# Decode attention with a gated MLP on one core: sums over d moved from VectorE to TensorE, K and V on one queue, MLP weights last

## The chip, the cores and the metric

The kernel runs on one core of a Trainium2 chip. The metric is the device time of one execution in microseconds (us). Each kernel is run several times beside the kernel before on the same chip; all runs quoted here are of the fast state (none lies over 1.5% above the fastest of its kernel), except two single looks whose state is unknown (they are marked). A profile is one more execution, recorded by the hardware profiler; its "span" is about 2 us shorter than the measured time.

Names: PE is TensorE, PEld its weight loads, DVE is VectorE, ACT is ScalarE, POOL is GpSimd, SP is the sync engine that issues DMA transfers. L327 is line 327 of the kernel.

## The reference, cut to what matters

```python
# B=2 sequences, one new token each; D=512, 32 heads, Sk=8192 cached positions, Dh=128, F=1376, bf16
h  = x + attention(layernorm(x), k_cache, v_cache, wq, wo)   # softmax(q k^T / sqrt(Dh)) v, per head
h2 = h + (relu(g) * u) @ W_down       # g, u = layernorm(h) @ W_gate, layernorm(h) @ W_up
```

There are 64 (sequence, head) pairs, called heads below. Each reads a K tile and a V tile of 2.1 MB and uses every element once. Together with wq, wo (4.2 MB each) and the MLP weights (4.2 MB), the core reads 281 MB.

## The kernel before

Position s = p*64 + j lies in partition p. For each head VectorE multiplies the K tile by q (copied to all partitions), then sums over d by halving: four tree adds down to 8 values per position and one reduce. ScalarE takes exp, and TensorE forms the weighted sum of V with 64 one-column matmuls.

```python
NB = 3                                    # three buffers for K (SP queue), three for V (ACT queue)
for i in range(NH):                       # 64 heads
    nc.vector.tensor_tensor(out=prod[:], in0=kt[buf][:], in1=qb, op=ALU.mult)        # L327
    # ... SP reloads kt[buf] for head i+3; wo is loaded at head 5
    while cur_w > 8:                      # 128 -> 64 -> 32 -> 16 -> 8
        half = cur_w // 2
        nc.vector.tensor_tensor(out=out_ap, in0=cur_in[:, :, 0:half],
                                in1=cur_in[:, :, half:cur_w], op=ALU.add)            # L349
        # ...
    nc.vector.tensor_reduce(out=scores[par][:], in_=cur_in, axis=AX.X, op=ALU.add)   # L358
    nc.scalar.activation(out=e_t[par][:], in_=scores[par][:], func=ACT.Exp, ...)
    for j in range(64):
        nc.tensor.matmul(O_ps[:, col:col + 1], lhsT=vt[buf][:, j, :], rhs=e_t[par][:, j:j + 1], ...)  # L377
# MLP weights go into K and V buffers freed near the end; then softmax sums, output projection of
# all 32 heads, layernorm, gate, up, down, a transpose to rows, store.
```

The softmax here doesn't subtract the row's maximum and nothing guards it: scores larger than these inputs give would overflow.

Of the kernel before, what the change touches and what calls it, by code (L numbers as in the profile page):

```python
# [13 lines left out]
class EngChain:  # L14

    def __init__(self, eng, sem):
        self.eng = eng
        self.sem = sem
        self.count = 0
        self.pending = False  # L20

    def wait(self):
        if self.pending:
            self.eng.wait_ge(self.sem, self.count)
            self.pending = False

    def run(self, inst):
        inst.then_inc(self.sem, 1)
        self.count += 1
        self.pending = True  # L30
        return inst


def bass_sequential_preLN__gqa_block_cached__glu_gated_reglu__decode_kernel(
# [11 lines left out]
):  # L46
    B, _, D = A_x.shape
    _, Hkv, Sk, Dh = A_k_cache.shape
    Hq = A_wq.shape[1] // Dh
    assert Hq == Hkv  # L50
    assert Dh == 128
    assert D % 128 == 0
    DC = D // 128
    J = Sk // 128
    assert Sk % 128 == 0 and J >= 2 and (J & (J - 1)) == 0
    F = B_W_gate.shape[1]
    FC = (F + 127) // 128
    NH = B * Hq
    inv_sqrt_dh = 1.0 / math.sqrt(Dh)
    eps = 1e-5  # L60
    qdim = Hq * Dh
    GH = 4 if Hq % 4 == 0 else Hq
    NGB = Hq // GH
    NG = B * NGB
    GW = GH * Dh
    assert GW <= 512
    NB = 3

    with ExitStack() as es:
# [3 lines left out]
        sem_x = S("x")  # L73
        sem_wo = S("wo")
        sem_wgu = S("wgu")
        sem_wd = S("wd")
        sem_prep = S("prep")
        sem_stats = S("stats")
        sem_lnx = S("lnx")
        sem_qps = S("qps")  # L80
        sem_qcopied = S("qcopied")
        kdone = [S(f"kdone{k}") for k in range(NB)]
        vdone = [S(f"vdone{k}") for k in range(NB)]
        multdone = S("multdone")
        sready = S("sready")
        expdone = S("expdone")
        pvdone = S("pvdone")
        sem_ident0 = S("ident0")
        sem_ident = S("ident")
        sem_z = S("ztok")  # L90
        sem_zinv = S("zinv")
        sem_zb = S("zb")
        sem_osb = S("osb")
        sem_attn = S("attn")
        sem_hprep = S("hprep")
        sem_hstats = S("hstats")
        sem_hn = S("hn")
        sem_gu = S("gu")
        sem_hd = S("hd")
        sem_y = S("ysem")  # L100
        sem_h2 = S("h2sem")
        sem_rows = S("rowsem")
        sem_rowsb = S("rowsbsem")
        osem = S("osem")
        dvesem = S("dvechain")
        sem_sq1a = S("sq1a")
        sem_sq1b = S("sq1b")
        sem_sq2a = S("sq2a")
        sem_sq2b = S("sq2b")

        dve = EngChain(nc.vector, dvesem)
        actsem = S("actchain")
        actc = EngChain(nc.scalar, actsem)

        kt = [es.enter_context(nc.sbuf_tensor(f"kt{i}", [128, J, Dh], BF16)) for i in range(NB)]
        vt = [es.enter_context(nc.sbuf_tensor(f"vt{i}", [128, J, Dh], BF16)) for i in range(NB)]
        wq_sb = es.enter_context(nc.sbuf_tensor("wq_sb", [128, DC, qdim], BF16))
        xrep = es.enter_context(nc.sbuf_tensor("xrep", [128, B * DC, 128], BF16))
        q_grp = [es.enter_context(nc.sbuf_tensor(f"qgrp{i}", [128, GW], BF16)) for i in range(2)]
        wo_sb = es.enter_context(nc.sbuf_tensor("wo_sb", [128, Hq, D], BF16))  # L120
        ones_f32 = es.enter_context(nc.sbuf_tensor("ones_f32", [128, 128], F32))
        ident_f32 = es.enter_context(nc.sbuf_tensor("ident_f32", [128, 128], F32))
        xT = es.enter_context(nc.sbuf_tensor("xT", [128, DC, B], BF16))
        xT_f = es.enter_context(nc.sbuf_tensor("xT_f", [128, DC * B], F32))
        xsq = es.enter_context(nc.sbuf_tensor("xsq", [128, DC * B], F32))
        sumb = es.enter_context(nc.sbuf_tensor("sumb", [128, B], F32))
        sumq = es.enter_context(nc.sbuf_tensor("sumq", [128, B], F32))
        mean = es.enter_context(nc.sbuf_tensor("mean", [128, B], F32))
        msq = es.enter_context(nc.sbuf_tensor("msq", [128, B], F32))
        var = es.enter_context(nc.sbuf_tensor("var", [128, B], F32))  # L130
        rstd = es.enter_context(nc.sbuf_tensor("rstd", [128, B], F32))
        vareps = es.enter_context(nc.sbuf_tensor("vareps", [128, B], F32))
        sqv = es.enter_context(nc.sbuf_tensor("sqv", [128, B], F32))
        lnxT = es.enter_context(nc.sbuf_tensor("lnxT", [128, DC, B], BF16))
        hT_f = es.enter_context(nc.sbuf_tensor("hT_f", [128, DC * B], F32))
        hsq = es.enter_context(nc.sbuf_tensor("hsq", [128, DC * B], F32))
        hnT = es.enter_context(nc.sbuf_tensor("hnT", [128, DC, B], BF16))
        hd = es.enter_context(nc.sbuf_tensor("hd", [128, FC * B], BF16))
        h2T_f = es.enter_context(nc.sbuf_tensor("h2T_f", [128, DC * B], F32))
        rows_sb = es.enter_context(nc.sbuf_tensor("rows_sb", [DC * B, 128], BF16))  # L140
        zinv = es.enter_context(nc.sbuf_tensor("zinv", [1, NH], F32))
        ZP = es.enter_context(nc.sbuf_tensor("ZP", [128, NH], F32))
        zb_sb = es.enter_context(nc.sbuf_tensor("zb_sb", [128, NH], F32))
        u_sb = es.enter_context(nc.sbuf_tensor("u_sb", [128, FC * B], F32))
        O_sb = es.enter_context(nc.sbuf_tensor("O_sb", [128, Hq, B], BF16))
        prod = es.enter_context(nc.sbuf_tensor("prod", [128, J, Dh], BF16))
        tb1 = es.enter_context(nc.sbuf_tensor("tb1", [128, J * 64], BF16))
        scores = [es.enter_context(nc.sbuf_tensor(f"scores{i}", [128, J], F32)) for i in range(2)]
        e_t = [es.enter_context(nc.sbuf_tensor(f"e{i}", [128, J], BF16)) for i in range(2)]

        if DC * F <= J * Dh and FC * D <= J * Dh and NH >= 3:
            alias_w = True
            pstride = kt[0][:].ap[0]
            wg_view = bass.AP(kt[(NH - 3) % NB], 0, [[pstride[0], 128], [F, DC], [1, F]])
            wu_view = bass.AP(kt[(NH - 2) % NB], 0, [[pstride[0], 128], [F, DC], [1, F]])
            wd_view = bass.AP(vt[(NH - 3) % NB], 0, [[pstride[0], 128], [D, FC], [1, D]])
        else:
            alias_w = False
            wg_t = es.enter_context(nc.sbuf_tensor("wg_sb", [128, DC, F], BF16))
            wu_t = es.enter_context(nc.sbuf_tensor("wu_sb", [128, DC, F], BF16))  # L160
            wd_t = es.enter_context(nc.sbuf_tensor("wd_sb", [128, FC, D], BF16))
            wg_view = wg_t[:]
            wu_view = wu_t[:]
            wd_view = wd_t[:]

        qps = es.enter_context(nc.psum_tensor("qps", [128, 2 * 512], F32))
        work = es.enter_context(nc.psum_tensor("work", [128, 512], F32))
        O_ps = work[:, 0:NH]
        zrow_ps = work[0:1, 64:64 + NH]
        zb_ps = work[:, 128:128 + NH]  # L170
        msum_ps = work[:, 192:192 + DC * B]
        e2_ps = work[:, 200:200 + DC * B]
        attnT_ps = work[:, 208:208 + DC * B]
        hsum_ps = work[:, 216:216 + DC * B]
        hsq_ps = work[:, 224:224 + DC * B]
        g_ps = work[:, 232:232 + FC * B]
        u_ps = work[:, 254:254 + FC * B]
        yT_ps = work[:, 276:276 + DC * B]
        rows_ps = work[0:DC * B, 288:288 + 128]

        NWQ = NGB
        sem_wq = [S(f"wq{k}") for k in range(NWQ)]
        nfull = F // 128
        frem = F - nfull * 128

        def dma_wq_chunk(k):
            return nc.sync.dma_start(  # L187
                wq_sb[:, :, k * GW:(k + 1) * GW],
                A_wq[:, k * GW:(k + 1) * GW].rearrange("(c p) n -> p c n", p=128),
            ).then_inc(sem_wq[k], 16)  # L190

        def dma_k(i):
            b, h = divmod(i, Hq)
            return nc.sync.dma_start(  # L194
                kt[i % NB][:], A_k_cache[b, h].rearrange("(p j) d -> p j d", p=128)
            ).then_inc(kdone[i % NB], 16)
# [7 lines left out]
        def emit_q_group_pe(g):  # L204
# [4 lines left out]
            if g >= 2:  # L209
                nc.tensor.wait_ge(sem_qcopied, g - 1)  # L210
# [9 lines left out]
        def emit_q_group_copy(g):  # L220
            slot = g % 2
            nc.scalar.wait_ge(sem_qps, g + 1)
            if g >= 2:
                nc.scalar.wait_ge(multdone, (g - 1) * GH)
# [321 lines left out]
```

## Time and profile before

| | before |
|---|---|
| time | 710.18 us (median of 4) |
| K multiply starts: head 0, 1, 61, 63 | 27.4, 41.6, 658.8, 678.8 us |
| end of the span | 708.4 us |

From the page of the kernel before: busy time of each engine; then, in 40 slices of 17.7 us, the busy share in tenths of VectorE and of the DMA engines, and the rate; then the line of instruction fetches (packets, MB, share).

```profile
span 708.4 us, 9878 instructions
PE 158.7 (22%) x4433; PEld 130.2 (18%) x4433; DVE 630.6 (89%) x424; ACT 34.4 (5%) x149; POOL 0.7 (0%) x6
DVE  0679998299999999999999999999999999999982
DMA  9999999999999999999999999999999999999940
GB/s 345 367 426 427 425 417 392 423 396 384 426 424 421 421 418 427 409 409 424 420 425 422 422 413 424 422 412 423 428 427 409 420 424 417 420 417 416 401 162 3
q8 instruction: 35, 0.57, 0.3%
```

VectorE and DMA are both busy nearly all the time. The rate is low in the first two slices, and in the slice that begins 35 us before the end loading is nearly over while VectorE still works. The chain of work that ended last, by engine, says which of the two rules:

```profile
DVE 84%; DMA 8%; SPq 4%; PE 2%; issue 2%; DVEq 0%; ACT 0%
```

One head in the middle of the run (timeline: start, duration, engine, line, operation):

```profile
338.57 4.43 DVE L327 TENSOR_TENSOR prod<-kt,qgrp 128x8192 bf16<-128x8192 bf16 x1
343.04 2.29 DVE L349 TENSOR_TENSOR tb<-prod 128x4096 bf16<-128x4096 bf16 x1
345.36 1.22 DVE L349 TENSOR_TENSOR prod<-tb 128x2048 bf16<-128x2048 bf16 x1
346.62 0.69 DVE L349 TENSOR_TENSOR tb<-prod 128x1024 bf16<-128x1024 bf16 x1
347.34 0.42 DVE L349 TENSOR_TENSOR prod<-tb 128x512 bf16<-128x512 bf16 x1
347.80 0.69 DVE L358 TENSOR_REDUCE scores<-prod 128x64 f32<-128x512 bf16 x1
348.58 4.43 DVE L327 TENSOR_TENSOR prod<-kt,qgrp 128x8192 bf16<-128x8192 bf16 x1
```

VectorE works without a gap: 10.0 us from one K multiply to the next. A head moves 4.19 MB, so this alone allows 419 GB/s. The 16 KB packets of the trace mostly take 611 ns on each of 16 DMA engines, or 429 GB/s. The two limits are 2 to 3% apart.

### The profile page before, as it was taken

The page shows a single profiled execution, that of the slowest core. Times are in us where ns is not written, and L with a number is a line of the kernel's source. Part 1 is how long each engine was busy: PE and PEld are TensorE (multiplying, and loading weights), DVE is VectorE, ACT ScalarE, POOL GpSimd, SP SyncE. Part 2 cuts the span into 40 slices and gives each one's busy share as a digit, 9 for nine tenths or more (in the row PEclk, how much of TensorE's full clock was granted, in tenths as well). Part 3 has the DMA queues.
Part 4 walks back from the last instruction along what each step waited for, and adds up shares of the span by engine and source line. Part 5 has one row for each costly group of instructions (what it writes and reads, how often), then busy time and mean ns, then how long its engine had stood idle before and what let it go on. Part 6 is the DMA issues. An engine that isn't in the chain of part 4 may idle for free.

```text
span 708.4 us, 9878 instructions
## 1 busy us (share of the span) xinstructions
PE 158.7 (22%) x4433; PEld 130.2 (18%) x4433; DVE 630.6 (89%) x424; ACT 34.4 (5%) x149; POOL 0.7 (0%) x6
## 2 busy tenths in 40 slices
PE   0221322011323132212322132122322232112215
PEld 0111222011222122212221122112221222112215
DVE  0679998299999999999999999999999999999982
ACT  0100000000000000000000000000000000000010
POOL 0000000000000000000000000000000000000000
DMA  9999999999999999999999999999999999999940
GB/s 345 367 426 427 425 417 392 423 396 384 426 424 421 421 418 427 409 409 424 420 425 422 422 413 424 422 412 423 428 427 409 420 424 417 420 417 416 401 162 3
DMA packets 30346, 281.70 MB, mean 398 GB/s; under 512 B 3328, under 2 KB 12896, under 8 KB 13920
## 3 DMA queue, kind: packets, MB, share of 16 engines
q1 hardware_dynamic: 21088, 146.84, 49.9%
q10 hardware_dynamic: 9216, 134.22, 46.1%
q8 instruction: 35, 0.57, 0.3%
q14 instruction: 7, 0.06, 0.0%
HBM read 281.05 MB, written 0.00 MB: 397 GB/s over the span
## 4 chain that ended last, share of the span: by engine, by line
DVE 84%; DMA 8%; SPq 4%; PE 2%; issue 2%; DVEq 0%; ACT 0%
DVE prod L327 38%; DVE tb L349 25%; DVE prod L349 14%; DMA kt<-in_A_k_cache_dram 8%; DVE scores L358 6%; SPq L194 2%; SPq L187 2%; PE work L422 1%; PE work L377 0%; PE work L464 0%; DVEq L323 0%; PE work L470 0%; PE work L494 0%; SPq L247 0%; ACT e L363 0%
## 5 line engine op out<-in xcount | busy, mean ns | idle before, releaser
L327 DVE TENSOR_TENSOR prod<-kt,qgrp 128x8192 bf16<-128x8192 bf16 x64 | 283.3, 4426 | 29.5 <-DMA kt<-in_A_k_cache_dram 20.8
L377 PE MATMUL work<-e,vt 128*128 128x1 bf16 x4096 | 119.5, 165 | 517.7 <-ACT e L363 517.7
L377 PEld LDWEIGHTS work<-e,vt 128*128 128x128 bf16 x4096 | 114.3, 104 | 535.2 <-ACT e L363 535.2
L349 DVE TENSOR_TENSOR tb<-prod 128x4096 bf16<-128x4096 bf16 (+1 forms) x128 | 190.9, 1491 | 4.4
L349 DVE TENSOR_TENSOR prod<-tb 128x2048 bf16<-128x2048 bf16 (+1 forms) x128 | 105.6, 825 | 4.4
L363 ACT ACTIVATE e<-scores 128x64 bf16<-128x64 f32 x64 | 16.4, 256 | 630.8 <-DVE scores L358 630.8
L358 DVE TENSOR_REDUCE scores<-prod 128x64 f32<-128x512 bf16 x64 | 43.9, 686 | 2.2
L213 PE MATMUL qps<-wq_sb,xrep 128*128 128x512 bf16 x64 | 29.9, 623 | 4.4 <-DVEq L303 3.3
L262 DVE CAST xT_f<-xT 128x8 f32<-128x8 bf16 x1 | 0.2, 172 | 19.0 <-DMA xT<-in_A_x_dram 19.0
L363 ACT ACTIVATION_READ_ACCUMULATOR e<-scores 128x1 f32 x64 | 11.9, 186 | 0.0
L213 PEld LDWEIGHTS qps<-wq_sb,xrep 128*128 128x128 bf16 x64 | 6.9, 128 | 14.2 <-issue 8.8
L226 ACT ACTIVATE qgrp<-qps 128x512 bf16<-128x512 f32 x16 | 9.3, 579 | 4.0 <-PE qps L213 4.0
L268 PE MATMUL work<-xT_f,ones_f 128*128 128x8 f32 x2 | 0.6, 372 | 20.4 <-DVE xsq L264 20.4
L268 PEld LDWEIGHTS work<-xT_f,ones_f 128*128 128x128 f32 x2 | 0.5, 310 | 20.4 <-DVE xsq L264 20.4
L422 PE MATMUL work<-O_sb,wo_sb 128*128 128x2 bf16 x128 | 3.6, 165 | 0.6 <-DVEq L416 0.6
L422 PEld LDWEIGHTS work<-O_sb,wo_sb 128*128 128x128 bf16 x128 | 3.5, 104 | 0.8 <-DVEq L416 0.8
L427 DVE TENSOR_TENSOR hT_f<-work,xT_f 128x8 f32<-128x8 f32 x1 | 0.2, 167 | 3.7 <-PE work L422 3.7
L475 DVE COPY u_sb<-work 128x20 f32<-128x20 f32 x1 | 0.2, 178 | 3.1 <-PE work L470 3.1
L403 DVE RECIPROCAL zinv<-work 1x64 f32<-1x64 f32 x1 | 0.5, 547 | 2.6 <-PE work L399 2.6
L464 PE MATMUL work<-hnT,kt 128*128 128x2 bf16 (+1 forms) x44 | 1.5, 170 | 2.1 <-DVEq L457 2.1
L464 PEld LDWEIGHTS work<-hnT,kt 128*128 128x128 bf16 (+1 forms) x44 | 1.5, 112 | 2.2 <-DVEq L457 2.2
L470 PE MATMUL work<-hnT,kt 128*128 128x2 bf16 (+1 forms) x44 | 1.5, 170 | 0.0
(53 smaller groups left out, 21.0 us busy)
## 6 DMA issues: line engine op xcount, KB each, us to landing
vt<-in_A_v_cache_dram ACTq DMA_DIRECT2D x64, 2048.0 KB, 13.0
kt<-in_A_k_cache_dram SPq DMA_DIRECT2D x64, 2048.0 KB, 13.6
wq_sb<-in_A_wq_dram SPq DMA_DIRECT2D x8, 512.0 KB, 11.4
wo_sb<-in_A_wo_dram SPq DMA_DIRECT2D x1, 4096.0 KB, 41.8
kt<-in_B_W_gate_dram SPq DMA_DIRECT2D x1, 1376.0 KB, 10.9
kt<-in_B_W_up_dram SPq DMA_DIRECT2D x1, 1376.0 KB, 6.5
vt<-in_B_W_down_dram SPq DMA_DIRECT2D x1, 1280.0 KB, 9.0
vt<-in_B_W_down_dram SPq DMA_DIRECT2D x1, 96.0 KB, 9.2
```

The lines of the kernel that those rows point to most:

```text
L187: return nc.sync.dma_start(wq_sb[:, :, k * GW:(k + 1) * GW], A_wq[:, k * GW:(k + 1) * GW].rearrange("(c p) n -> p c n", p=128),).then_inc( ...
L194: return nc.sync.dma_start(kt[i % NB][:], A_k_cache[b, h].rearrange("(p j) d -> p j d", p=128)).then_inc(kdone[i % NB], 16)
L213: last = nc.tensor.matmul(qps[:, slot * 512:slot * 512 + GW], lhsT=xrep[:, b_g * DC + c, :], rhs=wq_sb[:, c, col0:col0 + GW], start=(c == ...
L226: actc.run(nc.scalar.activation(out=q_grp[slot][:], in_=qps[:, slot * 512:slot * 512 + GW], func=ACT.Copy))
L327: nc.vector.tensor_tensor(out=prod[:], in0=kt[buf][:], in1=qb, op=ALU.mult).then_inc(multdone, 1)
L349: dve.run(nc.vector.tensor_tensor(out=out_ap, in0=cur_in[:, :, 0:half], in1=cur_in[:, :, half:cur_w], op=ALU.add))
L358: nc.vector.tensor_reduce(out=scores[par][:], in_=cur_in, axis=AX.X, op=ALU.add).then_inc(sready, 1)
L363: nc.scalar.activation(out=e_t[par][:], in_=scores[par][:], func=ACT.Exp, scale=inv_sqrt_dh, accum_out=ZP[:, col:col + 1]).then_inc(expdon ...
L377: last = nc.tensor.matmul(O_ps[:, col:col + 1], lhsT=vt[buf][:, j, :], rhs=e_t[par][:, j:j + 1], start=(j == 0), stop=(j == NJ - 1))
L422: last = nc.tensor.matmul(attnT_ps[:, ncx * B:(ncx + 1) * B], lhsT=wo_sb[:, h, ncx * 128:(ncx + 1) * 128], rhs=O_sb[:, h, :], start=(h == ...
L464: last = nc.tensor.matmul(g_ps[0:fw, fc * B:(fc + 1) * B], lhsT=wg_view[:, c, fc * 128:fc * 128 + fw], rhs=hnT[:, c, :], start=(c == 0), s ...
L470: last = nc.tensor.matmul(u_ps[0:fw, fc * B:(fc + 1) * B], lhsT=wu_view[:, c, fc * 128:fc * 128 + fw], rhs=hnT[:, c, :], start=(c == 0), s ...
```

## The change

The intent is to take the tree off VectorE so that DMA alone sets the pace, and to leave less behind the last load. The sums over d become matmuls with an identity, which add up in PSUM. K and V tiles share one ring of six slots and one queue. wq is loaded in one transfer of long rows. The MLP weights come last, after the last V, so that they land while the attention of the last head finishes. The outputs are formed in rows, which spares the final transpose but repeats the output projection in row form. To shorten the end, the projection of heads 0 to 27 is done before the weighted sum of head 61.

```diff
-    NB = 3
+    NB = 6
+        ring = [T(f"ring{i}", [P, J, Dh], BF16) for i in range(NB)]      # K and V in turn, all on SP
 # ...
-                    nc.vector.tensor_tensor(out=prod[:], in0=kt[buf][:], in1=qb, op=ALU.mult)
-                    while cur_w > RW_STOP:                               # tree adds on VectorE
-                        # ...
+                    for j0, j1 in parts:                                 # two halves of the tile
+                        t = dve.run(nc.vector.tensor_tensor(
+                            out=prod[:, j0:j1, :], in0=kt[:, j0:j1, :], in1=qb..., op=ALU.mult))
+                        for w in range(Dh // W8):                        # 16 matmuls of 256 columns
+                            mm = nc.tensor.matmul(
+                                S8[par][:, j0 * W8:j1 * W8], lhsT=ident[:],
+                                rhs=prod[:, j0:j1, w * W8:(w + 1) * W8],
+                                start=(w == 0), stop=(w == Dh // W8 - 1))
+                    summed[i] = dve.run(nc.vector.tensor_reduce(out=scores[par][:], in_=S8[par]..., ...))
 # ...
+                    if i == NH - 3:
+                        norm_batch(0, HA)          # softmax sums and output projection of heads 0 to 27
+                    # ... then the weighted sum of head i
+                    if i == NH - NB // 2 - 1:      # head 60: all K and V tiles are issued
+                        # ... W_gate, W_up, W_down on the same queue
 # ...
+                        for c in range(DC):        # gate and up, every tenth column of the weight
+                            lhsT = w[:, c, k:KF * P:KF] if k < KF else w[:, c, KF * P:F]
```

## The prediction

> **What bounds the kernel now.** Two limits lie almost on top of each other. The chain of waits is 84% DVE. From about 150 us on, every head takes 10.0 us (start to start of the K multiply in that chain), of which DVE is busy 9.74: multiply 4.43, four tree adds 2.29 + 1.22 + 0.69 + 0.42, reduce 0.69 (timeline). A head moves 4.19 MB, so DVE holds DMA to 419 GB/s. DMA could do little more: the trace's 16 KB packets mostly take 611 ns on each of 16 engines, which is 429 GB/s, and stretches not held by DVE (60 to 90 us) ran at 426. The rest is at the ends. The first 40 us run at 342 and 389 GB/s (table of windows; wq in 1 KB pieces, 2-byte x pieces, x landing after 18.6 us). At the end the last DVE multiply starts at 678.8, DMA is nearly idle from 683, and 25 us of DVE, attention and MLP work follow with nothing to load.
>
> **What the change does.** The four tree adds (4.62 us of DVE a head) become 32 identity matmuls of 256 columns. DVE keeps about 4.5 (multiply in halves) + 0.7 (reduce, now from PSUM). PE today runs 512 columns in about 0.43 us (wq matmuls: 4 in 1.89 us).[...] Per head that is 6.8 us[...], plus 1.87 for PV. In series: PV, first half, second half, reduce, handoffs:[...] about 10.2[...] compute drops below the 9.83 us that DMA needs per head, and the loop becomes DMA-bound.
>
> One queue instead of two should cost nothing: at 140 to 148 us the SP queue alone moved 430 GB/s[...]. Six slots give about 15 us of slack.
>
> **The sum.** DMA: 128 tiles at 4.92 us = 629.5; wq in long pieces 9.8 (was 12); wo still in 1 KB pieces 12.0; start about 3 us. So the last V lands near 655, and the MLP weights (4.2 MB) near 665. Behind the last V: PV 2, last projection and norm 5, gate and up 3 (1.5 each today), then down 2 to 4, output 2 (1.9 today). The end is near 671 to 672 of span; the measured time is 1.8 over the span today. The MLP weights hide under the attention tail, or the other way round; the tail after V costs about 17 us where today about 27 follow the last K/V use.
>
> So of about 36 us: about 10 to 15 from the loop (419 to 426 GB/s), about 5 from the start, the rest from the tail.
>
> Predicted 674 us, range 666 to 688; faster by over 2% 0.93, same 0.06, slower 0.01.
>
> **Right if:** DMA at 424 to 429 GB/s in every slice from the second to the last two, except where wo passes; DVE busy about 50%; DVE multiplies wait for DMA landings for some 2 to 4 us a head; last weight landing within 10 us of the end.
>
> **Wrong if:** [...] the wait of the DVE reduce on PE fills the head, heads take over 10 us, and the time goes to 685 to 700. Or a single queue leaves gaps between transfers (packets fewer than 16 in flight). Or the tail chain, with many small hops, is longer than I counted.

The last V lands at 629.5 + 9.8 + 12.0 + 3 = 654.3, given as 655; with 17 for the tail the span ends near 672, and with the 1.8 between span and measured time that is the 674 predicted. The 9.8 and 12.0 are estimates: in the kernel before a packet of 16 KB mostly takes 611 ns and one of 1 KB 49 ns, which give 9.8 and 12.5 for the 4.2 MB of wq or wo. What is cut is a faster rate of TensorE than the measured 0.43 us per 512 columns, with the times that followed from it; no trace of the kernel before shows it. The step from 10.2 us a head (estimate from the measured rate) to less than 9.83, and so to a loop bound by DMA, rested on that assumption alone.

## The result, and the profile after

The changed kernel takes 689.09 us (median of 4; 688.03 to 690.38) beside 710.18 us: 3.0% faster, where 5.1% was forecast. The time lies above the range of 666 to 688. The ratio is 0.9705, with an interval of 0.9691 to 0.9719. Such ratios are the mean time of one kernel's fast runs over that of the other's of the same rounds, so they are not quite the ratio of the medians quoted.

The same lines of the page, and the granted TensorE clock:

```profile
span 686.6 us, 14013 instructions
PE 499.0 (73%) x6626; PEld 384.0 (56%) x6626; DVE 340.9 (50%) x238; ACT 38.3 (6%) x213; POOL 0.7 (0%) x6
DVE  2545533544555455445635554564455445545631
PEclk9988986989888666678667668787778767668886
DMA  8999999999999999999999999999999999999980
GB/s 350 429 426 427 429 372 430 423 428 427 426 427 429 426 427 426 429 427 428 426 426 425 428 426 428 428 425 426 427 426 427 426 430 425 428 427 428 417 322 29
q8 instruction: 52, 0.85, 0.5%
```

```profile
DMA 77%; DVE 15%; PE 7%; issue 1%; ACT 0%; SPq 0%; DVEq 0%
```

VectorE is busy half as long, DMA runs at 425 to 430 GB/s in nearly every slice, and the chain is now DMA: the loop became what was predicted. A head in the middle:

```profile
299.67 4.49 DVE L324 TENSOR_TENSOR prod<-ring,q_all 128x4096 bf16<-128x4096 bf16 x2
299.99 1.76 PE L360 MATMUL O_ps<-e,ring 128*128 128x1 bf16 x64 [1.17 <-ACT O_raw L305]
302.02 4.85 PEld L329 LDWEIGHTS S_1<-prod,ident 128*128 128x128 bf16 x32 [0.37 <-DVE prod L324]
307.19 0.69 DVE L336 TENSOR_REDUCE scores<-S_1 128x64 f32<-128x512 f32 x1 [3.03 <-PE S_1 L329]
309.47 4.49 DVE L324 TENSOR_TENSOR prod<-ring,q_all 128x4096 bf16<-128x4096 bf16 x2 [1.58 <-DMA ring<-in_A_k_cache_dram]
```

The multiply of 4.49 us and the reduce of 0.69 are as foreseen. The 32 identity matmuls take 5.13 us from first to last. VectorE then waits 1.58 us for a K tile to land: heads are 9.8 us apart.

So where did the time come from, and where did the rest of the expected gain go? The starts of the K multiplies cut both runs into stretches:

| stretch | before | after | gained |
|---|---|---|---|
| start to multiply of head 1 | 41.6 | 28.6 | 13.0 |
| head 1 to head 61 | 617.2 | 608.5 | 8.7 |
| head 61 to head 63 | 20.0 | 25.4 | -5.4 |
| head 63 to the end of the span | 29.6 | 24.1 | 5.4 |

More than half of the gain is at the start. The loop gave less than 9 us of 617, as two limits so close together allow. The last two stretches, in which the prediction had put the largest part, cancel. The timeline of that end:

```profile
646.20 3.90 PE L273 MATMUL qps<-O_sb,wo_sb 128*128 128x2 bf16 x112 [1.29 <-DVE O_sb L294]
650.03 3.15 PE L279 MATMUL rows<-wo_sb,O_sb 128*2 128x128 bf16 x112
653.11 0.79 PE L360 MATMUL O_ps<-e,ring 128*128 128x1 bf16 x25
655.52 1.12 PE L360 MATMUL O_ps<-e,ring 128*128 128x1 bf16 x39 [1.61 <-issue]
656.49 5.32 PE L329 MATMUL S_0<-prod,ident 128*128 128x256 bf16 x32
...
662.46 4.55 DVE L324 TENSOR_TENSOR prod<-ring,q_all 128x4096 bf16<-128x4096 bf16 x3
...
671.00 1.74 PE L360 MATMUL O_ps<-e,ring 128*128 128x1 bf16 x64
...
676.79 2.82 PE L403 MATMUL S_0<-hn,big 128*128 128x2 bf16 x44 [2.02 <-DVE hn L228]
...
684.29 0.65 SPq L433 DMA_DIRECT2D out_dram<-o_rows  x1
```

The work of TensorE comes in the order in which the program lists it: first it projects 28 heads (L273 in column form, L279 in row form, 7 us together). Only then come the weighted sum of head 61 (L360) and the identity matmuls of head 62 (L329). VectorE waits for those (10.6 us before its reduce of head 62, L336), so the multiply of head 63 starts at 662.5 instead of about 656. The last weighted sum starts at 671.0. Gate takes 2.82 us for 44 matmuls (the kernel before: 1.54).

A second thing is seen in the DMA rows of the same stretch (40 slices of 1.2 us):

```profile
DMA  9999999999999999997544544411000000000000
GB/s 423 403 423 406 416 434 413 420 423 389 390 389 406 408 423 414 409 376 292 248 202 211 225 189 199 201 58 41 0 0 0 0 0 0 0 0 14 1 1 0
```

From about 662 us the engines move only about 200 GB/s, half the rate, for 10 us, although everything left to load was issued long before (the last issue is at 648 in the timeline). In the trace's DMA records (a packet is in flight from its start to its end; one per engine makes 16) there are 16 packets in flight until 662, then about 8 until 671; the last load ends at 673.1. By that count half of the engines are done about 10 us before the others, and the kernel waits for the last packet of a tile: the landing of the last weight is signalled at 673.6.

### The profile page after: what moved, and what is told of

It reads as the page before. It is cut to its first block, busy times and chain, and to the rows that moved or that the text cites. A ratio compares the mean times of both kernels' runs of the same rounds, so it can differ in the third digit from the quotient of the medians.

```text
span 686.6 us, 14013 instructions
## 1 busy us (share of the span) xinstructions
PE 499.0 (73%) x6626; PEld 384.0 (56%) x6626; DVE 340.9 (50%) x238; ACT 38.3 (6%) x213; POOL 0.7 (0%) x6
## 4 chain that ended last, share of the span: by engine, by line
DMA 77%; DVE 15%; PE 7%; issue 1%; ACT 0%; SPq 0%; DVEq 0%
DMA ring<-in_A_k_cache_dram 77%; DVE prod L324 14%; PE S_1 L329 2%; PE S_0 L329 2%; PE qps L273 1%; PE O_ps L360 1%; PE rows L279 0%; PE S_0 L403 0%; PE S_1 L403 0%; DVE scores L336 0%; PE rows L424 0%; SPq L159 0%; ACT e L339 0%; ACT q_all L257 0%; PE small L205 0%
## 5 line engine op out<-in xcount | busy, mean ns | idle before, releaser
L324 DVE TENSOR_TENSOR prod<-ring,q_all 128x4096 bf16<-128x4096 bf16 x129 | 287.7, 2272 | 101.6 <-DMA ring<-in_A_k_cache_dram 98.2
L329 PE MATMUL S_0<-prod,ident 128*128 128x256 bf16 x1024 | 176.5, 354 | 60.9 <-DVE prod L324 60.9
L329 PE MATMUL S_1<-prod,ident 128*128 128x256 bf16 (+1 forms) x1040 | 176.9, 352 | 44.6 <-DVE prod L324 44.6
L329 PEld LDWEIGHTS S_0<-prod,ident 128*128 128x128 bf16 x1024 | 126.6, 127 | 105.4 <-DVE prod L324 65.6
L329 PEld LDWEIGHTS S_1<-prod,ident 128*128 128x128 bf16 x1040 | 126.6, 126 | 88.8 <-DVE prod L324 48.4
L360 PE MATMUL O_ps<-e,ring 128*128 128x1 bf16 x4096 | 113.3, 164 | 61.0 <-ACT O_raw L305 59.1
L360 PEld LDWEIGHTS O_ps<-e,ring 128*128 128x128 bf16 x4096 | 107.8, 96 | 81.7 <-ACT O_raw L305 79.0
L336 DVE TENSOR_REDUCE scores<-S_0 128x64 f32<-128x512 f32 x32 | 22.1, 692 | 117.3 <-PE S_0 L329 117.3
L336 DVE TENSOR_REDUCE scores<-S_1 128x64 f32<-128x512 f32 x32 | 22.1, 692 | 109.9 <-PE S_1 L329 109.9
L250 PE MATMUL qps<-big,xrep 128*128 128x512 bf16 x64 | 17.3, 394 | 9.3 <-DMA big<-in_A_wq_dram 9.3
L257 ACT ACTIVATE q_all<-qps 128x512 bf16<-128x512 f32 x16 | 9.4, 587 | 10.0 <-PE qps L250 10.0
L305 ACT ACTIVATE O_raw<-O_ps 128x1 f32<-128x1 f32 x63 | 9.5, 151 | 0.0
L273 PE MATMUL qps<-O_sb,wo_sb 128*128 128x2 bf16 x128 | 4.8, 173 | 2.9 <-DVE O_sb L294 2.6
L273 PEld LDWEIGHTS qps<-O_sb,wo_sb 128*128 128x128 bf16 x128 | 4.5, 118 | 3.2 <-DVE O_sb L294 2.8
L279 PE MATMUL rows<-wo_sb,O_sb 128*2 128x128 bf16 x128 | 3.7, 299 | 0.0
L279 PEld LDWEIGHTS rows<-wo_sb,O_sb 128*2 128x2 bf16 x128 | 3.1, 118 | 0.0
## 6 DMA issues: line engine op xcount, KB each, us to landing
big<-in_A_wq_dram SPq DMA_DIRECT2D x1, 4096.0 KB, 12.6
```

The lines of the kernel that those rows point to most:

```text
L250: mm = nc.tensor.matmul(qps[g % 2][:, 0:GW], lhsT=xrep[:, b * DC + c, :], rhs=wq_sb[:, c, gb * GW:(gb + 1) * GW], start=(c == 0), stop=(c ...
L257: qcopied[g] = act.run(nc.scalar.activation(out=q_all[:, g, :], in_=qps[g % 2][:, 0:GW], func=ACT.Copy))
L273: mm = nc.tensor.matmul(attn_ps[:, c * B:(c + 1) * B], lhsT=wo_sb[:, h, c:D:DC], rhs=O_sb[:, h, :], start=(h == 0 and c == 0), stop=(h == ...
L279: mm = nc.tensor.matmul(rows[32 * g:32 * g + B, 0:P], lhsT=O_sb[:, h, :], rhs=wo_sb[:, h, g * P:(g + 1) * P], start=(h == 0), stop=(h == H ...
L305: ocopied[i] = act.run(nc.scalar.activation(out=O_raw[:, h * B + b:h * B + b + 1], in_=O_ps[i % 2][:, 0:1], func=ACT.Copy))
L324: t = dve.run(nc.vector.tensor_tensor(out=prod[:, j0:j1, :], in0=kt[:, j0:j1, :], in1=qb.unsqueeze(1).broadcast_to([P, j1 - j0, Dh]), op=A ...
```

## The experiments

Two theories stood at the start, each for a part of the missing time. Theory A: the tail is late because TensorE does the 28-head projection ahead of the last heads. Its rival: the last MLP weight ends the run anyway. Theory B: half of the DMA engines are late because they also fetch instructions, mostly TensorE's. Its rivals: some engines are slower by themselves, or are slowed by the compute engines.

| run | edit | time (us, median) | mean against the changed kernel's 689.1 |
|---|---|---|---|
| e1_spread | projection spread out | 684.97 | -4.2 |
| e2_contig | adjacent weight columns | 686.68 | -2.2 |
| e3_tree | tree on VectorE again | 697.23 | +8.2 |
| e4_two_queues | V on the ACT queue | 691.96 | +3.0 |
| e5_fetch | idle instructions on GpSimd | 702.53 | +12.8 |
| e6_weights_early | MLP weights at head 20 | 700.22 | +11.2 |
| e7_onepart | one part per head | 709.08 | +20.0 |
| f1_combo | e1 and e2 | 680.26 | -8.9 |
| f2_w16 | f1, 16 matmuls a head | 679.50 | -9.6 |
| g2_order | f2, last head reordered | 678.29 | -10.7 |
| g1_quarter_pv | f1 with a quarter of the V matmuls (wrong sums) | 677.96 | -11.6 |
| f3_wqhalf | f1, wq in 16 small transfers | 748.90 | +58.6 |
| d1_loads | loads only (wrong result, single run) | 667.56 | |
| d2_loads_fetch | loads and satisfied waits (wrong result, single run) | 686.79 | |

### The order on TensorE: e1_spread, e6_weights_early

```diff
-                    if i == NH - 3:
-                        norm_batch(0, HA)
+                    if i >= Hq + 5 and (i - Hq - 5) % 4 == 0 and i - Hq - 5 < HA:
+                        norm_batch(i - Hq - 5, i - Hq - 1)
```

> The changed kernel, but the output projection of heads 0 to 27 is done four heads at a time during the last 28 heads, not in one piece of 7 us in front of the last three heads. Theory A (the tail is long because TensorE, working in order, does that piece before the weighted sum of head 61, so heads 62 and 63 are late): the K multiply of head 63 starts at about 656 instead of 662.5 us, the last weighted sum starts within 2 us of the landing of the last V (about 663) instead of at 671, and the span falls by 5 to 7 us, to about 680. Rival (the end is set by the last MLP weight, which lands at about 672.6): at most 2 us of change.

It took 684.97 us, ratio 0.9645 (0.9631 to 0.9659) against 0.9705 for the changed kernel. The timeline of its last head:

```profile
655.24 4.56 DVE L324 TENSOR_TENSOR prod<-ring,q_all 128x4096 bf16<-128x4096 bf16 x3 [0.49 <-ACT O_raw L305]
657.59 6.47 PE L329 MATMUL S<-prod,ident 128*128 128x256 bf16 x48 [0.63 <-DVE prod L324]
...
666.55 1.83 PE L360 MATMUL O_ps<-e,ring 128*128 128x1 bf16 x64
```

The multiply of head 63 starts at 655.2, as expected. The last weighted sum starts at 666.6, which is 3.5 us after the last V and not within 2: the 48 identity matmuls before it took 6.47 us, while TensorE was granted 0.56 of its clock (table of windows, 657.6 to 664.1 us). So theory A holds against its rival, which allowed 2 us at most, but the gain of 4.2 us falls short of the 5 to 7 that it forecast.

The other side of it loads the MLP weights at head 20:

```diff
-                    if i == NH - NB // 2 - 1:
+                    if i == 20:
```

> The changed kernel with the MLP weights loaded at head 20 instead of last. Then K and V end about 10 us later (last V at about 672.6 instead of 663), the 28-head projection piece on TensorE still comes before the last heads but nothing is left to load behind them. Theory A (the tail is set by the piece on TensorE, not by the weights): the last weighted sum starts at about 676 to 681 and the time rises by 3 to 8 us. If the weights' landing is what ends the changed kernel, the time stays within 2 us.

It rose by 11 us to 700.22, more than the 3 to 8 expected. The last load of any kind ended at 672.8, yet the last weighted sum began only at 683.4 (forecast: 676 to 681) and the span ended at 699.0:

```profile
683.40 1.74 PE L360 MATMUL O_ps<-e,ring 128*128 128x1 bf16 x64
```

With nothing left to load, 26 us still followed. The weights' landing is therefore not what ended the changed kernel, and loading them last is worth about the 10 us that they take.

### The strided weight columns: e2_contig

```diff
-                        lhsT = w[:, c, k:KF * P:KF] if k < KF else w[:, c, KF * P:F]
+                        lhsT = w[:, c, k * P:k * P + n]
-                        wd_dram = B_W_down[0:KF * P, :].rearrange("(p k) n -> p k n", p=P)
+                        wd_dram = B_W_down[0:KF * P, :].rearrange("(k p) n -> p k n", p=P)
```

> The changed kernel, but the gate and up matmuls load their weights from adjacent columns instead of every tenth column, and the down weight is loaded in rows of 1 KB to match. If the stride is what makes these 88 matmuls take 5.5 us (64 ns each) where the kernel before took 3.0 us (34 ns each), they take about 3 us again and the span falls by 2.5 us. Rival (the half clock of TensorE in that stretch is the cause): they stay at 5.5 us and the span stays within 0.5 us.

It took 686.68 us, 2.2 us less in the mean; the intervals of the ratios just touch (0.9654 to 0.9693, against 0.9691 to 0.9719), so the proof is in the trace. One weight load fell from 157 to 104 ns, and in f1_combo, which has the same edit, gate and up together show:

```profile
669.57 2.94 PE L403 MATMUL S<-hn,big 128*128 128x2 bf16 x88 [2.02 <-DVE hn L228]
```

That is 2.94 us for 88 matmuls at a granted clock of 0.50, where the changed kernel had 5.50 at the same 0.50. The stride was the cause, not the clock.

### Where half of the DMA engines lose 10 us: d1_loads, d2_loads_fetch, e5_fetch, e7_onepart, f2_w16, f3_wqhalf, g1_quarter_pv

The page lists instruction fetches as packets of queue 8. For the changed kernel it counts 6626 matmuls and as many weight loads on TensorE, 13252 instructions, and 52 packets of 16 KB: one for every 255 instructions. The kernel before has 8866 and 35, one for every 253. So the fetches on queue 8 go with TensorE's instructions. Whether they cost the loads anything was the question.

The loads alone, in the same order, each slot reused once its tile has landed:

```diff
-                    # multiply, identity matmuls, exp, weighted sum, MLP
+                for t6 in range(2 * NH):
+                    freed[t6] = (ring_sem[t6 % NB], 16 * (t6 // NB + 1))     # freed by landing
```

> Wrong result on purpose: the same loads as the changed kernel on the same queue, in the same order, with a slot reused as soon as its tile has landed; no attention, no MLP, a zero output. 52 fetches shrink to a handful. Theory B (instruction fetches make half of the engines lag): all 16 engines finish within about 2 us of each other and the last load lands at about 661 us. Rival (some engines are slower by themselves): the last 10 us still run at half rate and the last load lands near 671. A third possibility, that the compute engines slow some DMA engines, looks like theory B here and is told apart by the next run.

```profile
DMA  9999999999999999995000000000000000000000
GB/s 423 382 430 406 399 434 420 423 430 400 369 394 431 404 440 393 423 398 219 0 1 0 0 0 0 0 0 0 0 0 0 0 0 0 0 0 0 0 0 0
```

The half-rate stretch is gone: the engines work at full rate until 662 and stop together (fewer than 14 packets in flight from 662.1, the last load ends at 662.9). This excludes engines that are slow by themselves. Then 100 satisfied waits per head were added on TensorE's queue:

```diff
+                    pe.need(freed[tk])
+                    for _ in range(100):
+                        nc.tensor.wait_ge(s_x, 16)
```

> The loads alone as in the run before, plus 100 already satisfied waits per head on the TensorE queue (6300 instructions, about 25 fetches), still no matmul and no vector work. Theory B: part of the engines lag again, by about 5 us, and the last load lands 3 to 5 us later than without them. If compute is what slows some engines: no difference.

```profile
q8 instruction: 12, 0.20, 0.1%
```

There were 12 fetches, not 25 (the page counts 3374 instructions in all, so about two waits went into one). The last load ended at 665.7 instead of 662.9, with no compute at all. That is just short of the 3 to 5 us, at half of the fetches; and as nothing is computed here, the compute engines are not what slows the late ones. (Its time of 686.79 us is TensorE working off its waits and says nothing here.)

With idle instructions on GpSimd in the whole kernel:

```diff
+                    for _ in range(128):
+                        nc.gpsimd.wait_ge(s_x, 16)
```

> The changed kernel with 128 waits per head that are already satisfied, on the idle GpSimd queue: 8192 more instructions, which do nothing but have to be fetched (the trace shows 52 fetches of 16 KB for 14013 instructions, so about 32 more). Theory B (the DMA engines finish up to 10 us apart because each fetch costs one engine about 1.5 us of its queue, and only some engines serve fetches): 84 or so fetches, the engines end about 6 us further apart (if the same half serves them) and the time rises by 3 to 6 us; or, if GpSimd is served by other engines, the lag moves and the time changes by less than 2 us. Rival (some engines are slower by themselves, or slowed by the compute engines): no change above 1 us.

```profile
q8 instruction: 52, 0.85, 0.5%
q14 instruction: 37, 0.30, 0.1%
```

Queue 14, with 5 packets in the changed kernel, has 37 now: 32 more, as forecast, but of 8 KB, for some 4100 instructions more on the page (18095 in all against 14013). The last load ended at 683.2, 10 us later, and in the last 10 us one packet was in flight: a single engine was behind. 32 blocks of 8 KB at the 611 ns that 16 KB take are 9.8 us (an estimate), so one engine seems to have served them all. The time rose by 12.8 us, more than the 3 to 6 expected for the same half. Nothing was computed by those instructions; they only had to be fetched and passed.

Two ways of having fewer matmuls were tried. The first drops the halves, with 16 matmuls of 512 columns per head:

```diff
-                    parts = last_parts if last else [(0, J // 2), (J // 2, J)]
+                    parts = last_parts if last else [(0, J)] if i < NH - 2 else [(0, J // 2), (J // 2, J)]
```

> The changed kernel, but each head except the last two is multiplied in one piece and summed with 16 identity matmuls of 512 columns instead of 32 of 256: about 2000 instructions fewer on TensorE (8 fetches fewer) and a longer head, since the sums cannot start at half. Theory B: the slow engines end about 1.5 us sooner, the time falls by 1 to 1.5 us as long as the loop stays bound by DMA. If TensorE is closer to its limit than I think, the heads take over 10 us and the time rises by over 5 us.

It lost 20 us: 709.08. Multiply (4.4), matmuls (5.1) and reduce (0.7) now follow one another, heads are 10.2 us apart, and the loop is no longer bound by DMA. With that the lag is gone too: 16 packets stay in flight until 675.7, 1.8 us before the last load ends, in spite of 44 fetches. The kernel before, with 35 fetches, shows the same (16 in flight until 682.2, the end at 683.3), and e3_tree below, with 36, comes near it (666.6 and 669.4). All three wait for compute; that this gives a late engine time to catch up is our reading.

The second keeps the halves and leaves 16 partial sums instead of 8 for VectorE:

```diff
-    W8 = 8
+    W8 = 16     # 8 matmuls of 512 columns per half, each half in a PSUM bank of its own
```

> f1_combo with the sums over d done by 16 identity matmuls of 512 columns a head (8 per half, 16 partial sums left for VectorE, which reduces each half by itself) instead of 32 of 256: about 2000 instructions and 8 fetches fewer, without giving up the overlap of the halves. Theory B: the lagging DMA engines end 1 to 1.5 us sooner and the time falls by 1 to 1.5 us against f1_combo. VectorE gets 0.7 us more per head, which is not critical. If fetches do not matter: no change, or 0.7 us slower in the last head.

The last load ended at 671.5 instead of 673.0, as forecast; the time went from 680.26 to 679.50. The intervals of the ratios (0.9567, 0.9553 to 0.9581, against 0.9578, 0.9564 to 0.9592) overlap, so the gain in time is likely but not shown.

To take away many fetches at once, three quarters of the V matmuls were left out in the first 61 heads. The sums are wrong (the result still passes the comparison):

```diff
-                    for j in range(J):
+                    js = range(J) if i > NH - 4 else range(0, J, 4)
+                    for j in js:
```

> Wrong result on purpose: f1_combo with only 16 of the 64 weighted-sum matmuls in the first 61 heads (the last three heads are whole, so the tail has the same work), about 5900 instructions fewer on TensorE, all loads the same. Theory B (each fetch of 16 KB of TensorE instructions costs the lagging engines about 0.2 us of the end: 662.9, 665.7, 671.5, 673.0 us with 0, 12, 44 and 52 fetches): about 29 fetches, the last load ends at about 668.5 instead of 673.0, the half-rate stretch at the end shrinks from 10 to about 5 us, and the time falls by 3 to 5 us to about 676. Rival (half of the engines lag for another reason, such as the work of the compute engines in general): the stretch stays near 10 us and the time within 1 us of f1_combo.

```profile
DMA  9999999999999999999655320000000000000000
...
q8 instruction: 4, 0.07, 0.5%
```

(The last line is for the window; the whole run has 29 fetches.) The last load ended at 668.7, and the half-rate stretch shrank from 10.7 to 6.0 us. The time fell by 2.7 us in the mean, a little short of 3 to 5 (the intervals, 0.9535 to 0.9566 against 0.9564 to 0.9592, just touch); the profiled span fell by 3.7. The runs with the same loads then stand so:

| run | fetches on queue 8 | fewer than 14 packets in flight from | last V lands | last load ends |
|---|---|---|---|---|
| d1_loads | 0 | 662.1 | 653.4 | 662.9 |
| d2_loads_fetch | 12 | 662.5 | 656.1 | 665.7 |
| g1_quarter_pv | 29 | 662.7 | 658.8 | 668.7 |
| f2_w16 | 44 | 662.2 | 661.7 | 671.5 |
| changed kernel | 52 | 662.1 | 663.6 | 673.1 |

(A landing is signalled about 0.5 us after its last packet ends.) The early engines do not move. The late ones end about 0.2 us later per fetch (10.2 us over 52). If eight engines share the fetches, as the eight packets in flight suggest, each fetch costs its engine 8 x 10.2 / 52 = 1.6 us (an estimate); a fetch packet itself is recorded with 1.08 us, a data packet of the same size with 0.61. Which engines these are, the trace doesn't say.

The last attempt was to give the other engines the wq load, so as to balance them:

```diff
-                nc.sync.dma_start(wq_sb, wq_dram).then_inc(s_wq, 16)
+                for m in range(P // 8):
+                    nc.sync.dma_start(wq_sb[8 * m:8 * m + 8], wq_dram[8 * m:8 * m + 8]).then_inc(s_wq, 16)
```

> f1_combo with wq loaded by 16 transfers of 8 partitions, which I expect to run on 8 of the 16 DMA engines only. If those 8 are the ones that do not serve the fetches, the others get 10 us of lead at the start, lose it to the fetches over the run, all engines end together at about 667 us and the time falls by about 5 us. If they are the ones that serve the fetches, the lag doubles to about 20 us and the time rises by about 5 us. If the transfers run on all 16 engines, little changes. Either way it shows whether the lag of half of the engines is a matter of bytes and queue time.

It failed, and answered nothing about the lag: 748.90 us, where 5 us less, 5 us more or little change was forecast. wq took about 79 us, and in that time the rate was (busy time of each engine, clock, DMA share, GB/s):

```profile
40.00:60.00 20.00, 0.00 (x0) 0.00 (x0) 0.00 (x0) 0.00 (x0) 0.00 (x0) 1.00 1.05 98
```

4.19 MB in 79 us are 53 GB/s. That these transfers would use eight of the engines was the expectation; the trace agrees: from 10 to 80 us its DMA records hold eight packets of wq (32 KB each) and eight of K and V (16 KB) in flight. But both kinds were slow: a wq packet took 5.0 us in the mean and one of K or V 2.6, where f1_combo has 1.3 and 0.61. Each transfer of the edit writes only eight partitions; whether that is the reason, no run tests.

### What each part of the change is worth: e3_tree, e4_two_queues

```diff
-                        for w in range(Dh // W8): # identity matmuls
+                    while w > W8:                 # tree adds on VectorE, as before
+                        t = dve.run(nc.vector.tensor_tensor(
+                            out=dst, in0=cur[:, :, 0:half], in1=cur[:, :, half:w], op=ALU.add))
```

> The changed kernel with the sums over d on VectorE as before (four tree adds and a reduce); queue, ring, weights last and row outputs stay. VectorE is bound again at about 10.0 us a head: 64 heads take 641 us from the first K landing at about 19 us, so the last head is summed at about 660 us, and the tail of about 16 us behind it gives a span of 676 to 684. If the sums on TensorE are what the change gains from, this run is slower than the changed kernel (690 or more). If they gain little, because DMA holds both at almost the same rate and the tail pile-up on TensorE is gone, it is as fast or faster by up to 8 us.

697.23 us: slower than the changed kernel by 8 us, and faster than the kernel before by 13. So the sums on TensorE gave 8 us of 21; queue, ring, order of the loads and the ends gave the rest. (The multiply of head 63 started at 667.1; the tail behind it was 28 us, not 16.)

```diff
-            nc.sync.dma_start(ring[s][:], cache(t)).then_inc(ring_sem[s], 16)
+            q, eng = (act, nc.scalar) if t % 2 else (sp, nc.sync)
+            eng.dma_start(ring[s][:], cache(t)).then_inc(ring_sem[s], 16)
```

> The changed kernel with the V tiles issued on the ACT queue and the K tiles on the SP queue. One queue costs nothing: within 2 us of the changed kernel. If the single queue is what costs, 5 us or more faster. If the order of landings matters (K and V interleaved, each landing later), the tail gets 2 to 5 us longer.

691.96 us, 3 us slower than one queue, and the last load ends at the same 673.3. The rate in the loop is the same with two queues and with one: from the 10th to the 37th of 40 slices 424 to 431 GB/s here, 425 to 430 in the changed kernel. What the single queue brings is order: with two, V tiles share the engines with x and wq at the start, wq lands after 22.3 us instead of 12.6, and the first multiply starts at 33.4 instead of 18.9. Most of that is caught up; at head 61 the run is 2.9 us behind.

### Together, and a last attempt: f1_combo, g2_order

> The two repairs that worked, together: output projection spread over the last 28 heads (4.1 us alone), adjacent weight columns (2.4 us alone). If they are independent the time is about 682.6. If the last weight landing (about 672.6 us) now ends the chain, they add up to less, 684.

680.26 us, 8.9 us less than the changed kernel, where the two edits alone give 6.4. The extra 2.5 us can be a matter of the clock: in the profiled run the 48 identity matmuls of the last head took 3.71 us at full granted clock, in e1_spread's 6.47 at 0.56. That was seen in one profile each and not tested.

g2_order starts from f2_w16:

```diff
-                    if last:
-                        norm_batch(HA, HB)       # heads 28 to 30, ahead of the last weighted sum
+                    # last weighted sum first; then project_t(HA, HB), project_t(Hq - 1, Hq), project_rows(HA, Hq)
```

> f2_w16 with the last head's weighted sum ahead of the projection of heads 28 to 30, whose row form comes after the column form of all four heads. If the order still costs: the weighted sum starts at about 662.9 instead of 663.9 us and the time falls by 0.6 to 1 us. If the landing of the last V holds it: no change.

678.29 us, ratio 0.9554 (0.9540 to 0.9568). The last weighted sum started at 663.8, not at 662.9, so the mechanism expected did not appear, and the interval overlaps that of f2_w16 (0.9553 to 0.9581). Inconclusive. Both beat the kernel before by 4.3 to 4.5% and the changed kernel by about 1.5%, with correct results.

## Why the prediction was wrong, point by point

- *The bound before, and the loop becoming DMA-bound:* right. Nearly all slices at 424 to 430 GB/s, DVE 50% busy. Waits of VectorE for K landings were 98 us in all, 1.5 us a head, below the 2 to 4 forecast; the identity matmuls took about 5.3 us a head, less than the 6.8 estimated from the rate of the kernel before. Two rates were measured: four matmuls of 512 columns take 1.87 us in the kernel before and 1.03 us near 36 us here, at a granted clock of 1.0. In the changed kernel's trace the granted clock alternates between 1.0 and 0.5 (118 records, 59 of each). (The trace of the kernel before holds no clock records; the 1.0 that the tool gives for it says nothing.)
- *"One queue instead of two should cost nothing":* right (e4_two_queues); it even gains 3 us.
- *"About 5 from the start":* too small. The second multiply starts 13 us earlier. The term counted lost bytes, not how late the first q and K were.
- *"About 10 to 15 from the loop":* 8.7 up to head 61.
- *"The last V lands near 655, and the MLP weights near 665":* wrong, and the larger of the two failures. The last V landed at 663.6 and the last weight at 673.6, 13 us before the end of the span instead of the 10 given under "Right if". The sum divided all bytes by the mean rate of 16 engines. Loads alone did fit it (last V at 653.4, last load at 662.9); with 52 instruction fetches half of the engines, by the packets in flight, were 10 us later (the last load ended at 673.1), and the kernel waits for the last packet of a tile.
- *"The tail after V costs about 17 us":* wrong; it cost 23.0. "PV 2, last projection and norm 5" had about the right sizes (1.7 and 4.0), but the sum let the PV start when V lands, and it started 7.4 us later, at 671.0: 7 us of projection stood on TensorE in front of the last three heads (4 us, e1_spread). "Gate and up 3 (1.5 each today)" took a duration from contiguous weight columns for strided ones (2 us, e2_contig).
- *"The rest from the tail":* this was to be 16 to 20 us; the stretches from head 61 on gained nothing. "Wrong if" did name a tail chain "longer than I counted", but as many small hops, not as a queue of work in front of the last heads.

With both tail repairs the kernel takes 680.3, and with 23 fetches fewer 678.0, against 674 forecast. With the remaining 29 fetches the last load still ends 6 us later than with none (668.7 against 662.9); what part of the last 4 us this is, was not tested. Not settled is which DMA engines serve the fetches. Nor is it shown why the V matmuls of head 61 pause for 1.6 us after the 25th (653.9 to 655.5). It may be that TensorE itself waits for a fetch: a fetch packet of queue 8 runs from 653.2 to 654.3, and in e6_weights_early a pause of 1.7 us after the same 25th matmul (from 664.9) also follows the start of one (664.3 to 665.4).

## What to carry to other kernels

When a loop becomes bound by DMA, plan the end by the slowest of the 16 engines and not by the mean rate, and count instructions: here each fetch, one for about 255 TensorE instructions, put off the last load by 0.2 us (10.2 us over 52). Work moved forward "to shorten the tail" must still be placed in the order of the engine that does it: in front of the last heads 7 us of it held up everything behind. And before expecting much from relieving the busiest engine, see how far behind the next limit is: here 10.0 against 9.8 us a head.
